# Decode step with cached attention and a gated mixer: the query weights loaded as two halves on two DMA queues

## The chip, the cores and the metric

One core of a Trainium2 chip runs the kernel. The metric is the time of one execution on the device in microseconds; less is better. The engines are named by their tasks: TensorE (PE in the profile) multiplies matrices, VectorE (DVE) and ScalarE (ACT) work on elements, GpSimd (POOL) does small copies, and SyncE (SP) issues loads. SyncE and ScalarE each have a DMA queue of their own (q1 and q10 in the profile); both are served by the same 16 DMA engines of the core.

## The reference

One token, x of 1024 values, goes through two branches, and a scalar gate mixes them:

```
g = sigmoid(sum(x * gate_w))
q = x @ wq                               # wq 1024 x 4096: 32 heads of 128
a = softmax(q k^T / sqrt(128)) v @ wo    # 4 K/V heads, 65536 cached keys each; wo 4096 x 1024
z = gelu(x @ w_in)                       # w_in 1024 x 3584, split into z1 and z2
b = (z1 * (w_sp * layernorm(z2) + b_sp)) @ w_out     # w_out 1792 x 1024
out = g * a + (1 - g) * b
```

All inputs are bfloat16. The K and V caches are 64 MiB each (4 x 65536 x 128 values of two bytes); with the weights the kernel reads 162 MB.

## The kernel before

**Storage.** All big inputs go through one ring in on-chip memory: five slots of 16384 columns on 128 partitions (SUB = 16384; a column is one bfloat16). Slots 0 to 2 hold blocks of K, the last two, from column VB on, hold wq, then w_in, then w_out, then blocks of V; at the end wo takes the place of all.

**The stream.** `load` enters a transfer into the list `stream`, with the keys by which it is used, its place in the ring and its source. The list begins with wq (one load, 32768 columns: on each partition eight rows of wq, one behind the other, 64 KB), the K blocks 0 and 1 (one load of the same size), w_in (28672 columns, in the place of wq), K blocks 2 and 3, w_out, and then K and V by turns.

**The order of the issues.** `issue` walks along the list and stops at the first transfer whose place in the ring has not been used up. `done(key)` marks a transfer as used, and calls `issue` again. All transfers of the list are put on SyncE's queue, in the order of the list (line 389), and each has a semaphore. Four small loads, x, gate_w, w_sp and b_sp, are issued by ScalarE (`small`, line 288). `Recorder` works out from each step's reads and writes which semaphores it must wait for. Where a step waits, all later steps on its engine wait behind it. At the end, `emit` moves SyncE's first two loads (`R.ahead = 2`) and ScalarE's first four (`R.early = 4`) ahead of the barrier with which the program starts.

**The work around the change.** TensorE first transposes x (line 432), spreads w_sp and b_sp over the partitions (line 437), and sums for the gate (line 444). Then one step of 64 matmuls (lines 454 to 465; the instructions have lines 260 and 262) forms q from xT and wq. VectorE copies the result (line 467); two short steps (lines 471 and 479) and copies on VectorE (lines 474 and 482) turn it, and GpSimd writes it to qpad (line 490). From then on the loop over K blocks runs: each block is transposed by VectorE in four pieces (line 502) and multiplied with qpad on TensorE. VectorE's program has the transposes of K block 0 behind the copy of line 482. The issue of w_in stands on SyncE behind the end of the projection, since w_in takes the place of wq; every later load stands behind w_in.

Of the kernel before, what the change touches and what calls it, by code (L numbers as in the profile page):

```python
# [138 lines left out]
def bass_gated_mix__gqa_block_cached__mixer_gmlp__decode_kernel(  # L139
# [29 lines left out]
    SUB = 16384  # L169
# [15 lines left out]
    OFF = {}  # L185
# [16 lines left out]
    arena = nc.alloc_sbuf_tensor("arena", [128, NA], BF16)  # L202

    def ab(name, n, o=0):
        return arena[:, OFF[name] + o:OFF[name] + o + n]

    def af(name, n, o=0):
        return arena[:, OFF[name] + 2 * o:OFF[name] + 2 * (o + n)].bitcast(F32)
# [8 lines left out]
    xT, wb, wbb, oneb = ab("XT", KC), ab("WB", 2), af("WBB", 2), ab("ONEB", 128)  # L217
# [30 lines left out]
    ob, mb, fb = obt[:, :], mbt[:, :], fbt[:, :]  # L248
# [5 lines left out]
    R = Recorder()  # L254
    P = R.op

    def mm(e, loaded, *a, **kw):

        if not loaded:
            return e.matmul(*a, **kw)  # L260
        with nc.discard():
            one = e.matmul(*a, **kw).ins  # L262
        return e.add_instruction(dataclasses.replace(one, name=nc.get_next_instruction_name(), ldweights=False))
# [21 lines left out]
    def small(dst, src, key):  # L285
        def f(e):
            with nc.allow_non_contiguous_dma(reason="a few bytes"):
                return e.dma_start(dst, src)  # L288
        P("ACT", f, w=[key], dma="l" + key)
# [12 lines left out]
    stream = []  # L302
# [1 line left out]

    GRAN = 1024

    def load(keys, src, off):

        n = len(stream)
        w = src.shape[1]  # L310
        for i, key in enumerate(keys):
            place[key] = (n, off + i * (w // len(keys)), w // len(keys))
        stream.append((keys, off, src))

    def rows(w, i, c):

        return w[128 * c * i:128 * c * (i + 1), :].rearrange("(p c) n -> p (c n)", c=c)
# [9 lines left out]
    WQ_N = HQ * Dh  # L327
    VB = KR * SUB

    def load_k(n, slot):  # L330
        load([("k", n)], kv(A_k_cache, n), slot * SUB)

    def load_k2(n, slot):
        load([("k", n), ("k", n + 1)], kv(A_k_cache, n, True), slot * SUB)

    def load_v2(n, off):
        load([("v", n), ("v", n + 1)], kv(A_v_cache, n, True), off)

    load([("wq", 0)], rows(A_wq, 0, 8), VB)
    load_k2(0, 0)  # L340
    load([("win", 0)], rows(B_w_in, 0, 8), VB)
    load_k(2, 2)
# [22 lines left out]
    def store():  # L365
        P("SP", lambda e: e.dma_start(out[0, 0].rearrange("(q n) -> q n", n=QW), osrc), r=["orow"],
          w=["out"], dma="out")
# [5 lines left out]
    def grains(off, w):  # L373
        return list(range(off // GRAN, (off + w + GRAN - 1) // GRAN))

    def issue():

        while issued[0] < len(stream):
            n = issued[0]
            keys, off, src = stream[n]  # L380
            w = src.shape[1]
            gr = grains(off, w)
            if any(k not in used for x in gr if x in owner for k in owner[x]):
                return
            for j, x in enumerate(gr):
                owner[x] = (keys[j * len(keys) // len(gr)],)
            if n == len(stream) - 1:
                store()
            P("SP", lambda e, o=OFF["RING"] + off, w=w, src=src: e.dma_start(arena[:, o:o + w], src),  # L389
              w=[("slot", x) for x in gr], dma="s%d" % gr[0])  # L390
            issued[0] += 1

    def use(key):
        n, off, w = place[key]
        assert n < issued[0], key
        return arena[:, OFF["RING"] + off:OFF["RING"] + off + w], [("slot", x) for x in grains(off, w)]

    def done(key):
        used.add(key)
        issue()  # L400

    issue()


# [8 lines left out]
      r=["m32"], w=["sel"])  # L413
    P("DVE", lambda e: e.tensor_reduce(mq, vw(idf, 0, [[1, 16], [16, 8]]), AXX, ALU.add), r=["idf"], w=["mq"])
    P("DVE", lambda e: e.tensor_reduce(mhalf, vw(idf, 0, [[32, 2], [64, 2], [1, 32]]), mybir.AxisListType.XY, ALU.add),
      r=["idf"], w=["mhalf"])
# [4 lines left out]
    for fe in range(4):  # L421
        P("POOL", lambda e, fe=fe: e.tensor_copy(vw(sele, 128 * fe, [[32, 4], [1, 32]]),
                                                vw(idb, 64 * (fe // 2) + fe % 2, [[0, 4], [2, 32]])),
          r=["idb"], w=[KSE])
# [5 lines left out]
    def f(e):  # L430
        for c in range(KC):
            ins = e.matmul(tb[:, c:c + 1], vw(xm, c, [[8, 128]], 0, 8), oneb[0:8, 0:1], start=(c == 0),  # L432
                           stop=(c == KC - 1), skip_group_check=True)
        return ins
    P("PE", f, r=["xm", "oneb"], w=[KTB])
    P("DVE", lambda e: e.tensor_copy(xT, tb[:, 0:KC]), w=["xT", KTB])
    P("PE", lambda e: e.matmul(mb[:, 0:2], oneb[0:1, :], wb[0:1, :], start=True, stop=True),  # L437
      r=["oneb", "wsp", "bsp"], w=["mb"])
# [6 lines left out]
      r=["ones", "gs"], w=[KTB])  # L445
# [4 lines left out]
      r=["g"], w=["omg"])  # L450
    P("DVE", lambda e: e.tensor_scalar(mhalf, mhalf, col(C_G), None, op0=ALU.mult), r=["mhalf", "g"], w=["mhalf"])


    wqs, keys = use(("wq", 0))

    def f(e):
        for c in range(KC):
            for cg in range(4):
                for s in range(2):
                    o = WQ_N * c + 512 * (4 * s + cg)  # L460
                    ins = mm(e, s > 0, ob[32 * cg:32 * cg + 1, 512 * s:512 * (s + 1)], xT[:, c:c + 1], wqs[:, o:o + 512],
                                   start=(c == 0), stop=(c == KC - 1), tile_position=(0, 32 * cg),
                                   skip_group_check=True)
        return ins
    P("PE", f, r=["xT"] + keys, w=["ob"])
    done(("wq", 0))
    P("DVE", lambda e: e.tensor_copy(psb[0:97, :], ob[0:97, :]), w=["psb", "ob"])  # L467

    def f(e):
# [306 lines left out]
    store()  # L776

    R.ahead = 2
    R.early = 4
    R.emit(nc)  # L780


# [26 lines left out]
```

## Time and profile before

| | |
|---|---|
| median of 3 runs | 381.89 us (381.82 to 381.96) |
| the profiled execution | span 380.3 us from its first to its last instruction; no other time is recorded for it, and the median lies 1.6 us above the span |
| read from memory | 162.01 MB, 426 GB/s over the span |
| SyncE's DMA queue | 98.9% of 16 engines' span |
| ScalarE's DMA queue | 36 packets |
| TensorE, VectorE, ScalarE, GpSimd busy | 62%, 54%, 6%, 2% |

The busy shares are means over the span. The share of a DMA queue is the time that its packets took on the 16 DMA engines. "Issue to landing" of a load is the time from the issuing instruction to the moment at which its semaphore has its full count. Brackets behind an instruction give the idle time of its engine before it, and what ended that.

### The profile page before, as it was taken

How to read it: one execution, taken by the hardware profiler on the slowest of the kernel's cores; microseconds unless marked ns; L12 is line 12 of the kernel's file. 1: busy time of each engine (PE TensorE's matmuls, PEld its weight loads, DVE VectorE, ACT ScalarE, POOL GpSimd, SP SyncE). 2: the span in 40 equal slices, each digit the busy share in tenths (PEclk: the TensorE clock that was granted, in tenths of full speed). 3: DMA queues.
4: the chain of work that ended last, by engine and by line, in shares of the span. 5: the costliest groups of instructions: out<-in, count | busy, mean ns of one | idle time of the engine just before them, and what ended most of it. 6: DMA issues, size and time to landing. Idle time of an engine off the chain costs nothing.

```text
span 380.3 us, 2581 instructions
## 1 busy us (share of the span) xinstructions
PE 235.1 (62%) x1449; PEld 58.1 (15%) x836; DVE 204.6 (54%) x162; ACT 23.3 (6%) x24; POOL 8.4 (2%) x37
## 2 busy tenths in 40 slices
PE   0061388458558924895788138952895884739378
PEld 0010011011111200122112001220121110212015
DVE  4011496778389525965892249745774882312020
ACT  1000000010420000002200000022000000220000
POOL 5000000000000000000000000000000000000000
PEclk9998599696859985998699859995899697958689
DMA  9999999999999999999999999999999999999996
GB/s 435 427 420 400 469 388 438 441 469 431 401 414 441 441 443 427 434 410 424 477 441 434 434 434 414 415 441 441 434 407 433 445 441 441 436 403 424 419 426 262
DMA packets 4254, 162.17 MB, mean 426 GB/s; under 512 B 532, under 2 KB 532, under 8 KB 788
## 3 DMA queue, kind: packets, MB, share of 16 engines
q1 hardware_dynamic: 4208, 162.01, 98.9%
q8 instruction: 9, 0.15, 0.2%
q10 hardware_dynamic: 36, 0.00, 0.0%
q14 instruction: 1, 0.01, 0.0%
HBM read 162.01 MB, written 0.00 MB: 426 GB/s over the span
## 4 chain that ended last, share of the span: by engine, by line
DMA 56%; PE 23%; DVE 18%; ACT 1%; issue 1%; SPq 0%; ACTq 0%; DVEq 0%
DMA arena<-in_A_k_cache_dram 34%; DVE arena L502 15%; DMA arena<-in_A_wo_dram 10%; DMA arena<-in_A_v_cache_dram 8%; PE scp L260 7%; PE scp L262 6%; DMA arena<-in_B_b_sp_dram 5%; PE obt L260 4%; PE obt L262 4%; DVE arena L539 1%; PE fbt L712 1%; PE fbt L660 1%; ACT arena L534 1%; SPq L389 0%; ACTq L288 0%
## 5 line engine op out<-in xcount | busy, mean ns | idle before, releaser
L502 DVE STREAM_TRANSPOSE arena<-arena 128x2048 f32<-128x2048 f32 x64 | 143.0, 2284 | 48.2 <-DMA arena<-in_A_k_cache_dram 32.7
L260 PE MATMUL scp<-arena 128*128 128x512 bf16 (+1 forms) x275 | 112.8, 429 | 87.7 <-DVE arena L502 86.3
L262 PE MATMUL scp<-arena 128*128 128x512 bf16 (+1 forms) x279 | 113.1, 427 | 0.0
L260 PE MATMUL obt<-arena 128*64 128x512 bf16 (+2 forms) x334 | 62.9, 419 | 17.5 <-DMA arena<-in_A_v_cache_dram 17.5
L262 PE MATMUL obt<-arena 128*64 128x512 bf16 (+2 forms) x334 | 62.2, 414 | 0.0
L260 PEld LDWEIGHTS scp<-arena 128*128 128x128 bf16 (+1 forms) x275 | 27.7, 104 | 200.1 <-issue 101.3
L539 DVE STREAM_TRANSPOSE arena<-arena 128x2048 bf16<-128x2048 bf16 x7 | 16.2, 2311 | 28.5 <-PE obt L262 26.4
L534 ACT ACTIVATE arena<-arena 128x2048 bf16<-128x2048 f32 x8 | 16.0, 2002 | 218.6 <-DVE arena L531 195.6
L260 PEld LDWEIGHTS obt<-arena 128*64 128x64 bf16 (+1 forms) x334 | 18.3, 113 | 70.7 <-issue 56.1
L519 DVE TENSOR_SCALAR_CACHE_REDUCE arena<-scp 128x2048 f32<-128x2048 f32 x8 | 18.3, 2292 | 16.0 <-PE scp L262 16.0
L580 PE MATMUL mbt<-arena 128*128 128x128 bf16 x16 | 1.9, 258 | 12.6 <-DVE arena L575 12.6
L542 DVE STREAM_TRANSPOSE arena<-arena 128x1024 bf16<-128x1024 bf16 x2 | 2.5, 1246 | 12.7 <-PE obt L262 12.7
L490 POOL COPY arena<-arena 32x32 bf16<-32x32 bf16 x16 | 3.2, 203 | 234.5 <-PE scp L262 209.7
L568 DVE RECIPROCAL arena<-mbt 128x1 f32<-128x1 f32 x4 | 0.6, 139 | 14.1 <-PE mbt L563 14.1
L531 DVE TENSOR_REDUCE arena<-mbt 128x1 f32<-128x32 f32 x4 | 0.8, 192 | 13.5 <-PE mbt L528 13.5
L437 PE MATMUL mbt<-arena 1*128 1x2 bf16 x1 | 0.2, 158 | 12.3 <-DMA arena<-in_B_b_sp_dram 12.3
L439 DVE COPY arena<-mbt 128x2 f32<-128x2 f32 x1 | 0.2, 160 | 12.3 <-PE mbt L437 12.3
L775 DVE CAST arena<-fbt 36x128 bf16<-36x128 f32 x1 | 0.3, 283 | 11.0 <-PE fbt L712 11.0
L432 PE MATMUL scp<-arena 8*128 8x1 bf16 x8 | 0.7, 199 | 8.7 <-DVE arena L427 8.7
L712 PE MATMUL fbt<-arena 128*32 128x128 bf16 x128 | 4.1, 220 | 0.1
L712 PEld LDWEIGHTS fbt<-arena 128*32 128x32 bf16 x128 | 3.6, 97 | 1.6 <-DMA arena<-in_A_wo_dram 0.8
L467 DVE CAST arena<-obt 97x1024 bf16<-97x1024 f32 x1 | 1.2, 1225 | 4.9 <-PE obt L262 4.9
(91 smaller groups left out, 54.2 us busy)
## 6 DMA issues: line engine op xcount, KB each, us to landing
arena<-in_A_k_cache_dram SPq DMA_DIRECT2D x6, 4096.0 KB, 33.1
arena<-in_A_v_cache_dram SPq DMA_DIRECT2D x2, 4096.0 KB, 26.0
arena<-in_B_w_in_dram SPq DMA_DIRECT2D x1, 7168.0 KB, 30.4
arena<-in_A_wo_dram SPq DMA_DIRECT2D x3, 2048.0 KB, 33.4
arena<-in_B_w_out_dram SPq DMA_DIRECT2D x1, 3584.0 KB, 21.5
arena<-in_A_wo_dram SPq DMA_DIRECT2D x1, 1280.0 KB, 30.3
arena<-in_A_wo_dram SPq DMA_DIRECT2D x1, 512.0 KB, 31.0
arena<-in_A_wo_dram SPq DMA_DIRECT2D x1, 256.0 KB, 30.8
```

What stands on the lines that cost most here:

```text
L260: return e.matmul(*a, **kw)
L262: one = e.matmul(*a, **kw).ins
L467: P("DVE", lambda e: e.tensor_copy(psb[0:97, :], ob[0:97, :]), w=["psb", "ob"])
L490: P("POOL", lambda e, pb=pb: e.tensor_copy(vw(qpad, 24 + 32 * pb, [[QP, 4], [1, 8]], 32 * pb, 32), vw(qall, 8 * g, [[32, 4], [1, 8]], 32 * ...
L502: P("DVE", lambda e: e.transpose(ktb(i).bitcast(F32), sl[:, 4096 * p:4096 * (p + 1)].bitcast(F32)), r=keys[4 * p:4 * p + 4], w=[("kt", i % ...
L519: P("DVE", lambda e: e.tensor_scalar(scs(j), scp[:, :], 0.0, None, op0=ALU.add, op1=ALU.max, accum_out=maxc[:, j:j + 1]), w=[("sc", j % 2) ...
L534: P("ACT", lambda e: e.activation(psb2, scs(j), ACTF.Exp, bias=gcol(j // 2, K_NB), scale=SCALE, accum_out=lp[:, j:j + 1]), r=[("sc", j % 2 ...
L539: P("DVE", lambda e: e.transpose(ptsb2, psb2), r=["psb"], w=[("ptsb", 0), ("ptsb", 1)])
L542: P("DVE", lambda e: e.transpose(ptsb(n), ab("PSB", 1024, 1024 * (n % 2))), r=["psb"], w=[("ptsb", n % 2)])
L580: ins = e.matmul(mb[:, 0:128], sel[:, 128 * c:128 * (c + 1)], osc[:, 128 * c:128 * (c + 1)], start=(c == 0), stop=(c == 3))
L660: ins = e.matmul(fb[32 * b:32 * (b + 1), 0:QW], e4z[0:97, 31 - j:63 - j], part[0:97, QW * s:QW * (s + 1)], start=(first and s % (NW // 2) ...
L712: ins = e.matmul(fb[32 * b:32 * (b + 1), 0:QW], ovz[:, z:z + 32], sl[:, o:o + QW], start=False, stop=(i == 3 and c == 7), tile_position=(0 ...
```

## The change

The load of wq becomes two loads, each of half of the columns that a partition holds: the first four rows of wq on a partition (32 KB), and the next four. The first is issued by SyncE as before, at the head of its queue, followed by K blocks 0 and 1. The second is issued by ScalarE, behind its four small loads; `R.early` becomes 5, so that it too stands ahead of the barrier. The projection reads one half or the other according to the chunk `c`, remains one step, and waits for both halves.

```
-    def load(keys, src, off):
+    def load(keys, src, off, eng="SP"):
...
-        stream.append((keys, off, src))
+        stream.append((keys, off, src, eng))
...
-    load([("wq", 0)], rows(A_wq, 0, 8), VB)
+    for i, eng in enumerate(("SP", "ACT")):
+        load([("wq", i)], rows(A_wq, 0, 8)[:, SUB * i:SUB * (i + 1)], VB + SUB * i, eng)
...
-            P("SP", lambda e, o=OFF["RING"] + off, w=w, src=src: e.dma_start(arena[:, o:o + w], src),
+            P(eng, lambda e, o=OFF["RING"] + off, w=w, src=src: e.dma_start(arena[:, o:o + w], src),
               w=[("slot", x) for x in gr], dma="s%d" % gr[0])
...
-    wqs, keys = use(("wq", 0))
+    wqs, keys = zip(*(use(("wq", i)) for i in range(2)))
...
-                    o = WQ_N * c + 512 * (4 * s + cg)
-                    ins = mm(e, s > 0, ob[32 * cg:32 * cg + 1, 512 * s:512 * (s + 1)], xT[:, c:c + 1], wqs[:, o:o + 512],
+                    o = WQ_N * (c % 4) + 512 * (4 * s + cg)
+                    ins = mm(e, s > 0, ob[32 * cg:32 * cg + 1, 512 * s:512 * (s + 1)], xT[:, c:c + 1], wqs[c // 4][:, o:o + 512],
...
-    P("PE", f, r=["xT"] + keys, w=["ob"])
+    P("PE", f, r=["xT"] + keys[0] + keys[1], w=["ob"])
     done(("wq", 0))
+    done(("wq", 1))
...
-    R.early = 4
+    R.early = 5
```

More of the change, by code (lines that the diff above doesn't have):

```diff
@@ L379, in issue @@
             n = issued[0]
-            keys, off, src = stream[n]
+            keys, off, src, eng = stream[n]
             w = src.shape[1]
```

## The prediction

> **What bounds the kernel now.** I read the page first: shares, queues, the chain's totals. From the table of DMA queues and the lines on HBM traffic:
>
> ```profile
> DMA  9999999999999999999999999999999999999996
> ...
> q1 hardware_dynamic: 4208, 162.01, 98.9%
> ...
> HBM read 162.01 MB, written 0.00 MB: 426 GB/s over the span
> ```
>
> q1 is SyncE's queue. Its packets fill the core's 16 DMA engines for 98.9% of the span, while TensorE is busy 62% and VectorE 54%. The bound is the stream of 162 MB. The chain's DMA share of 56% is smaller only because the chain steps through instructions that release buffers while the stream runs anyway. An edit therefore costs time where it leaves the DMA engines without work, and saves time only where it takes idle time out, and 98.9% leaves little to take.
>
> Second, the timeline of the first 42 us, where the change sits (columns: start us, duration us, engine, line, what; in brackets the idle time before it and what ended it):
>
> ```profile
> 0.00 0.37 SPq L389 DMA_DIRECT2D arena<-in_A_wq_dram  x1
> 0.12 0.56 ACTq L288 DMA_DIRECT2D arena<-in_A_x_dram  x1
> 0.42 0.42 SPq L389 DMA_DIRECT2D arena<-in_A_k_cache_dram  x1
> ...
> 1.34 0.27 ACTq L288 DMA_DIRECT2D arena<-in_B_b_sp_dram  x1
> ...
> 7.42 1.22 DVE L427 TENSOR_TENSOR arena<-arena 8x1024 bf16<-8x1024 bf16 x1 [1.92 <-DMA arena<-in_A_x_dram]
> ...
> 21.67 0.16 PE L437 MATMUL mbt<-arena 1*128 1x2 bf16 x1 [12.32 <-DMA arena<-in_B_b_sp_dram]
> ...
> 28.93 0.33 SPq L389 DMA_DIRECT2D arena<-in_B_w_in_dram  x1
> ...
> 31.40 0.29 DVE L482 CAST arena<-scp 128x128 bf16<-128x128 f32 x1 [0.43 <-PE scp L479]
> ```
>
> ```profile
> 41.32 4.50 DVE L502 STREAM_TRANSPOSE arena<-arena 128x2048 f32<-128x2048 f32 x2 [9.63 <-DMA arena<-in_A_k_cache_dram]
> ```
>
> Two things are to be seen. The next big load, w_in, is issued at 28.93, when the projection's last matmul has ended; until then SyncE's queue holds only wq and the first K block, and that block lands at 41.32. So w_in waits in the queue for about 12.4 us: this is the cover. And bsp, two bytes, is issued at 1.34 and lands only at 21.5 (the chain gives it 20.19 us), while x, issued 1.2 us earlier, lands at 7.42.
>
> Third, the DMA view of the window from 0 to 42 us, which says why:
>
> ```profile
> q1 hardware_dynamic: 304, 17.69, 99.0%
> q10 hardware_dynamic: 36, 0.00, 0.1%
> ...
> arena<-in_B_w_in_dram SPq DMA_DIRECT2D x1, 7168.0 KB, 30.4
> ...
> arena<-in_A_wq_dram SPq DMA_DIRECT2D x1, 21.9
> ```
>
> q10 is ScalarE's queue. wq and the K block have 128 rows of 64 KB each; 304 packets are their 256 rows, 16 small ones for each of the two loads, and the first 16 of w_in. So a packet is one row of a load, and each engine has 8 of them from each big load. The 36 of q10 are twice 8+8+1+1: one for each row of x, gate, wsp and bsp, and one more behind each. A 64 KB packet takes (41.32-21.9)/8 = 2.43 us on an engine. From x to bsp lie six packets of q10 on the engine that carries bsp (two each of gate, wsp, bsp) and 21.53-7.42 = 14.1 us: 2.35 us for each. So an engine takes one packet of SyncE's queue, then one of ScalarE's, by turns, however small the latter is, and one engine (call it E0) carries a part of all four small loads: eight turns.
>
> **The change, part by part.** *SyncE.* The wq load shrinks from 64 KB to 32 KB a row and the K block moves up behind it. The count of SyncE's instructions is unchanged.
>
> *ScalarE.* One more load is issued behind the four small ones, at about 1.65 us for 0.37 us (the wq row). The first ScalarE work is the table load at 2.12; even 0.4 us more there is nothing, as its next work waits 19.8 us for TensorE. If that cover were gone it would cost these 0.4 us.
>
> *TensorE.* The same 64 matmuls in one step, now behind two semaphores ahead of the first matmul. The first half is not used early, so the step starts when the later half lands. Behind it stand the whole of TensorE's program, VectorE's L467, and on SyncE the w_in issue with every later load.
>
> *When the later half lands.* Take E0, with packets of 1.21 us (32 KB) and 2.42 us (64 KB). SyncE's first half needs 8 x 1.21 = 9.7 us, and its eight turns alternate with the eight packets of the small loads, so bsp is down at about 12 us instead of 21.5. Only then does ScalarE's half of wq begin on E0, and its opponent is now the K block: eight turns of 1.21 + 2.42 = 3.63 us, 29.0 us in all. 12 + 29 = 41. So the second half lands together with the K block, at about 41.3: the engine's bytes are the same as before, and the K block's landing does not move. An engine without small packets is done with wq at about 22 to 24 us, one with those of x and gate (four turns) at about 31; E0 is last and decides. The turn order leaves one uncertainty: if the last wq packet, with its small one, is through a turn sooner, ahead of the last K packet, it is 41.3-2.4 = 38.9. I take 41.3: before, bsp needed all eight turns, ending at 21.5 beside wq's own end at 21.9, and the same phase puts wq's end behind the eighth K packet.
>
> *What is late next.* The projection begins at 41.3 instead of 23.08, and the gate's chain (L437 to L444, 1.4 us, which now holds up the projection) is long done. From the first projection matmul to the w_in issue it is 28.93-23.08 = 5.85 us, with a slow first 4.2 us (0.43 us a matmul, later 0.22) that I keep: the first scoring matmuls at 43.77 also start slow for 4.2 us after idling. So w_in is issued at 47.15, when the DMA engines have stood empty since about 41.3. An issue into an empty queue needs time too: wq landed 21.9 us after issue, against 19.4 for the K block, the same bytes behind it: 2.5 us. w_in then takes what it took from the K block's landing on, 28.93+30.4-41.32 = 18.0 us, and lands at 47.15+2.5+18.0 = 67.65 against 59.33: 8.3 us late. Some of the 2.5 us is a spread between engines that the old 18.0 us also holds; with 2.0 it is 7.8. I take 8.1.
>
> *Does it stay?* Projection start to the end of L482 is 8.6 us, so the first K transposes start at 49.95 instead of 41.32: the consumers are 8.6 us late, the stream 8.1. The later loads are issued well ahead: the K issue at 79.62 is 7.7 us before w_out lands (65.81+21.5), the V issue at 99.59 about 7.1 us before the K block ahead of it lands (87.3+19.4); 0.5 us of relative delay fits. With the engines 98.9% full nothing later can give time back, as that needs faster transfers, not earlier issues. The same holds to the last wo load, behind which the tail is unchanged. So the whole 8.1 us reaches the end.
>
> The sum: the profiled span 380.3 + 8.1 = 388.4; the median of 381.89 lies 1.6 above the span, so 390.0.
>
> **A rule beside the rows.** The Trainium skill, "DMA: Bandwidth & Descriptors", section "Queues, rings and completion order", says that an engine goes round between queues packet by packet, and puts a typical packet at some 9 to 17 descriptors. The taking of turns agrees with the 2.35 us above; the size does not. If a turn were all nine descriptors of a load, x would have had to wait for all of wq and land near 21.9, and here it landed at 7.42, with a packet per row. By turns of nine the engine would do SyncE's half (9.7 us), x, the K block (19.4), and then, with SyncE's queue empty, the other small ones and ScalarE's half (9.7): again an end near 41 and a sum near 390, but with the K block down at about 31, ahead of wq; by single rows they land together.
>
> The same page, "Rules for kernel authors", speaks against the change as a way to bandwidth: loads from several issuing engines share the same DMA engines, and only issue time is saved. By that rule alone the sum would be no change, 381.9.
>
> **The rivals.**
>
> *No gap (not slower).* An engine shares by bytes, or E0 does not carry all four small loads. By bytes, ScalarE's half on E0 starts at 12 and goes at half rate: 2 x 9.7 = 19.4 us, landing at 31.4. It decides at 41.32-2.5-5.85 = 33.0: a landing before that leaves w_in queued in time, and the time stays 381.9. The consumers would start at 31.4+8.6 = 40.0, still ahead of the K block. Against it: two bytes took 20.19 us, which sharing by bytes would not do, and eight turns of 2.43 us fit that best. 9%.
>
> *One turn earlier.* The second half lands at 38.9; w_in is issued at 44.75 and lands 5.9 us late instead of 8.3. With the same half-microsecond doubt 5.4 to 5.9, so 387.3 to 387.8. 18%.
>
> *More than the gap.* The stream of smaller packets or the late consumers cost another 1 to 2 us, for instance a K or V issue that misses its turn because VectorE's backlog of eight transposes starts 8.6 us late: 391 to 392. Against it the 7 us that those issues are ahead. 8%.
>
> *Faster.* bsp lands 9 us earlier, which takes 1.4 us out ahead of the projection, and a better fill of the engines at the start might save some. The first has no worth, as the K block at 41.32 rules; the second is at most what is missing to 100% in the window, about 0.4 us of 42. 3%.
>
> The forecast itself, 389.4 to 390.6, has 62%.
>
> **How the numbers follow.** A difference of 0.2% (0.8 us) is about what the measurement can tell from none. Slower by more: 62+18+8 = 88%. Within: the 9% without a gap, less 1 for rounding up the faster case: 8%. Faster: 4%. The range runs from the earlier turn less half a microsecond, 386.8, to 391.6, into the case of more than the gap; it leaves out the cases without a gap and the outer part of the last, under 20%.
>
> **What would show it.** In the profile after: bsp lands at about 12 us and L437 runs there; the first projection matmul starts at 41 us, ended by a wait for wq; w_in is issued at about 47; the DMA share falls to near nothing between 41.5 and 48.5; the first transposes start at about 50; and every later landing is 8 us late. If the projection starts at 39 the turn was one earlier; before 33 and with no hole in the DMA row, I am wrong about the turns; a hole of 7 us without a longer span would mean that the stream has slack which 98.9% does not show.

## The result and the profile after

The changed kernel takes 390.0 us (median of 5 runs, 389.75 to 390.2), the one before 381.89 us (381.68 to 381.96) beside it: 1.0214 times as long, 95% interval 1.0204 to 1.0225. The forecast was 390.0 us. The span of the profiled execution grew from 380.3 to 388.7 us.

From the page of the changed kernel, the DMA row of the 40 slices (9.7 us each), the queues and the traffic:

```profile
DMA  9999289999999999999999999999999999999996
...
q1 hardware_dynamic: 4208, 157.82, 94.4%
q10 hardware_dynamic: 180, 4.20, 2.5%
...
HBM read 162.01 MB, written 0.00 MB: 417 GB/s over the span
```

The same bytes are read; 4.2 MB of them, ScalarE's half of wq, now go over q10. The row that was all nines has a 2 in its fifth slice, 39 to 49 us: the stream stops once, and nowhere else. Its place is seen in the timeline (start, duration, engine, line, what; idle time before, and what ended it):

```profile
1.75 0.36 ACTq L390 DMA_DIRECT2D arena<-in_A_wq_dram  x1
...
11.97 0.16 PE L438 MATMUL mbt<-arena 1*128 1x2 bf16 x1 [4.24 <-DMA arena<-in_B_b_sp_dram]
...
46.78 0.33 SPq L390 DMA_DIRECT2D arena<-in_B_w_in_dram  x1
...
49.25 0.29 DVE L484 CAST arena<-scp 128x128 bf16<-128x128 f32 x1 [0.43 <-PE scp L481]
49.46 4.50 DVE L504 STREAM_TRANSPOSE arena<-arena 128x2048 f32<-128x2048 f32 x2
```

b_sp (the prediction's bsp) is down at 11.8 us instead of 21.5, w_in goes out at 46.78 instead of 28.93, and the first K transposes start at 49.46 instead of 41.32, and no longer wait for a load: the K block had landed at 41.1. The chain of work that ended last has the half itself, and it has the first matmul of the projection right behind it:

```profile
1.75 39.14 DMA arena<-in_A_wq_dram
40.89 0.14 issue
41.03 0.60 PE obt L260 x4
```

Issued at 1.75, ScalarE's half lands at 40.9. The hole is in the windows of 2 us (the last two columns are the share of the DMA engines and GB/s, each packet being counted in the window in which it starts):

```profile
41.00:43.00 2.00, 1.97 (x20) 0.40 (x12) 0.00 (x0) 0.00 (x0) 0.00 (x0) 1.00 0.00 0
43.00:45.00 2.00, 2.00 (x24) 0.42 (x12) 0.00 (x0) 0.00 (x0) 0.00 (x0) 1.00 0.00 0
45.00:47.00 2.00, 1.72 (x32) 0.18 (x8) 0.22 (x1) 0.00 (x0) 0.00 (x0) 1.00 0.00 0
```

For six microseconds TensorE works (first column of busy time) and no packet starts. By the times of the single packets in the trace no DMA engine is busy from 40.7 to 47.7 us. The DMA view gives how long each load took from issue to landing:

```profile
arena<-in_B_w_in_dram SPq DMA_DIRECT2D x1, 7168.0 KB, 20.4
...
arena<-in_A_wq_dram SPq DMA_DIRECT2D x1, 4096.0 KB, 18.1
arena<-in_A_wq_dram ACTq DMA_DIRECT2D x1, 4096.0 KB, 39.1
```

Two loads of the same size, issued 1.75 us apart, land at 18.1 and 40.9 us. w_in lands at 46.78 + 20.4 = 67.2 us instead of 59.3: 7.9 us late. The K load issued at 79.62 before is issued at 87.46, the V load at 107.27 instead of 99.59, and the first loads of wo at 337.99 instead of 330.07: everything behind the hole is issued 7.7 to 8.0 us late to the end, but for one V load, which goes out 10.0 us late (220.81 instead of 210.77) without delaying what follows. In this execution another 0.4 us comes in the last part (the output is stored at 387.45 instead of 379.10); the medians differ by 8.1 us, and I don't read more into that 0.4.

### The profile page after: what moved, and what is told of

Read it like the earlier page. It is cut to its first block, busy times and chain, and to the rows that moved or that the text cites. A ratio compares the mean times of both kernels' runs of the same rounds, so it can differ in the third digit from the quotient of the medians.

```text
span 388.7 us, 2583 instructions
## 1 busy us (share of the span) xinstructions
PE 234.1 (60%) x1449; PEld 58.1 (15%) x836; DVE 204.4 (53%) x162; ACT 23.2 (6%) x24; POOL 9.3 (2%) x37
## 4 chain that ended last, share of the span: by engine, by line
DMA 65%; DVE 17%; PE 17%; issue 1%; ACTq 0%; SPq 0%; DVEq 0%
DMA arena<-in_A_k_cache_dram 38%; DVE arena L504 15%; DMA arena<-in_A_wq_dram 10%; DMA arena<-in_A_v_cache_dram 9%; DMA arena<-in_A_wo_dram 8%; PE scp L260 5%; PE scp L262 4%; PE obt L260 3%; PE obt L262 3%; DVE arena L541 1%; PE fbt L714 1%; ACTq L288 0%; DVE arena L577 0%; DVE arena L575 0%; SPq L390 0%
## 5 line engine op out<-in xcount | busy, mean ns | idle before, releaser
L504 DVE STREAM_TRANSPOSE arena<-arena 128x2048 f32<-128x2048 f32 x64 | 143.0, 2284 | 35.7 <-DMA arena<-in_A_k_cache_dram 22.1
L260 PE MATMUL scp<-arena 128*128 128x512 bf16 (+1 forms) x275 | 111.1, 420 | 75.8 <-DVE arena L504 75.5
L262 PE MATMUL scp<-arena 128*128 128x512 bf16 (+1 forms) x279 | 110.5, 415 | 0.0
L260 PE MATMUL obt<-arena 128*64 128x512 bf16 (+2 forms) x334 | 64.1, 425 | 47.1 <-DMA arena<-in_A_wq_dram 27.6
L262 PE MATMUL obt<-arena 128*64 128x512 bf16 (+2 forms) x334 | 63.5, 422 | 0.0
L582 PEld LDWEIGHTS mbt<-arena 128*128 128x128 bf16 x16 | 1.1, 114 | 13.6 <-DVE arena L577 13.6
## 6 DMA issues: line engine op xcount, KB each, us to landing
arena<-in_B_w_in_dram SPq DMA_DIRECT2D x1, 7168.0 KB, 20.4
arena<-in_A_wq_dram SPq DMA_DIRECT2D x1, 4096.0 KB, 18.1
```

The costliest lines, as they stand in the source:

```text
L504: P("DVE", lambda e: e.transpose(ktb(i).bitcast(F32), sl[:, 4096 * p:4096 * (p + 1)].bitcast(F32)), r=keys[4 * p:4 * p + 4], w=[("kt", i % ...
L582: ins = e.matmul(mb[:, 0:128], sel[:, 128 * c:128 * (c + 1)], osc[:, 128 * c:128 * (c + 1)], start=(c == 0), stop=(c == 3))
```

## The experiments

The theory: a DMA engine takes one packet, that is one row of a load, of each queue by turns. On the engine that carries all four small loads, ScalarE's half stands behind eight tiny packets, each of which costs it one of SyncE's packets, and then shares turns with K packets of twice its size. So it lands with the K block, and the issue of w_in, which hangs on it, comes after the engines have run out of work. Rivals: the split or the smaller rows cost by themselves; two queues with big loads slow the stream; engines share by bytes; the late projection costs through VectorE and TensorE. Each experiment is the changed kernel with one edit, unless it says otherwise; the kernel before, run beside them, took 381.8 to 381.9 us.

### The split without the second queue

```
-    for i, eng in enumerate(("SP", "ACT")):
+    for i, eng in enumerate(("SP", "SP")):
...
-    R.ahead = 2
-    R.early = 5
+    R.ahead = 3
+    R.early = 4
```

> Both halves of wq on SyncE's queue, one behind the other, ahead of the K block; the four small loads alone on ScalarE's. Theory of turns (ScalarE's half stands behind eight small packets on one DMA engine and then shares turns with the K block): wq lands at 21.5 to 22 us as before, no hole, 381.9 us within 0.5; bsp lands at about 12 us, because SyncE's packets are now 32 KB. Rival, the smaller packets or the two loads cost by themselves: something between 382.5 and 390.

Measured: 381.84 us, ratio 0.9999 (0.9990 to 1.0008). The projection's first matmul starts at 21.75 us and b_sp's matmul at 12.02. The split and the smaller rows cost nothing; they even let b_sp through early. So the loss does not come without the second queue.

### The small loads on SyncE's queue

The four small loads go to the head of SyncE's queue; the halves stay on two queues.

```
...
-    small(xrow[0:8, 0:128], A_x[0, 0].rearrange("(i n) -> i n", i=8), KX)
+    small(xrow[0:8, 0:128], A_x[0, 0].rearrange("(i n) -> i n", i=8), KX, "SP")
...
-    R.ahead = 2
-    R.early = 5
+    R.ahead = 6
+    R.early = 1
```

> The halves on two queues as in the change, but the four small loads go to the head of SyncE's queue, so that ScalarE's queue holds only its half of wq. Theory of turns: the half no longer stands behind eight small packets, both halves land by 22 to 24 us, w_in is issued by 30 us, no hole, 381.9 us within 0.5. Rival, two queues with big loads at once slow the stream or the half is late because ScalarE's queue is slow to start: the loss stays, 388 to 390.

Measured: 381.86 us, ratio 1.0000 (0.9991 to 1.0010). From its timeline:

```profile
22.09 0.60 PE L260 MATMUL obt<-arena 128*1 128x512 bf16 x4 [9.75 <-DMA arena<-in_A_wq_dram]
...
28.26 0.33 SPq L390 DMA_DIRECT2D arena<-in_B_w_in_dram  x1
```

Two queues with 4 MB each at once are as fast as one. What costs in the change is what stands ahead of the half in its own queue. Nor is it faster: the rule of the Trainium skill, "DMA: Bandwidth & Descriptors", section "Rules for kernel authors", that loads spread over issuing engines share the same DMA engines and gain no bandwidth, agrees with this 381.86.

### Fewer small packets ahead: six and four turns

b_sp, and in the second kernel w_sp too, are issued by GpSimd. The edit of the first of the two:

```
...
-    small(wb[0:1, 1:2], B_b_sp.rearrange("(a n) -> a n", a=1), "bsp")
+    small(wb[0:1, 1:2], B_b_sp.rearrange("(a n) -> a n", a=1), "bsp", "POOL")
...
-    R.early = 5
+    R.early = 4
```

> The change with one small load, b_sp, issued by GpSimd instead of ScalarE, so that six small packets instead of eight stand ahead of ScalarE's half on the engine that carries them all. Theory of turns: each turn fewer brings the landing forward by one 64 KB packet, 2.42 us, so 40.9 - 4.85 = 36.0 us; w_in is issued at 41.9 instead of 46.8 and the loss falls from 8.1 to about 3.2 us: 385.1 us, within 0.7. Rival, the loss hangs on two queues or on small packets as such: 389 to 390.

> The change with two small loads, w_sp and b_sp, issued by GpSimd, so that four small packets stand ahead of ScalarE's half on the engines that carry x and gate_w. Theory of turns: 40.9 - 4 x 2.42 = 31.2 us for the landing of wq, w_in issued at about 37, before the hole opens; 381.9 us within 0.6. Eight, six and four turns then give losses of 8.1, 3.2 and 0. Rival, the loss falls in proportion to the small packets: four turns would still lose half of it, 386.

Measured: 385.04 us with six turns (ratio 1.0084, 1.0069 to 1.0099), 381.84 us with four (1.0002, 0.9993 to 1.0012). The timeline of six, then of four:

```profile
36.13 0.60 PE L260 MATMUL obt<-arena 128*1 128x512 bf16 x4 [20.11 <-DMA arena<-in_A_wq_dram]
...
41.93 0.33 SPq L390 DMA_DIRECT2D arena<-in_B_w_in_dram  x1
```

```profile
31.60 0.60 PE L260 MATMUL obt<-arena 128*1 128x512 bf16 x4 [10.72 <-DMA arena<-in_A_wq_dram]
...
37.31 0.33 SPq L390 DMA_DIRECT2D arena<-in_B_w_in_dram  x1
```

The projection starts at 41.03, 36.13 and 31.60 us with eight, six and four turns: 4.9 and 4.5 us for two turns each, or 2.3 to 2.45 us a turn, where a 64 KB packet takes 2.43. The loss goes 8.1, 3.2, 0: not in proportion, since it begins only where w_in's issue is too late, and 2 bytes moved to another queue are worth 5 us here. With four turns the projection starts 8.5 us later than in the kernel before (31.60 instead of 23.08 us), and this costs nothing: w_in is out in time, and the transposes wait for the K block anyway.

### Smaller K packets

K blocks 0 and 1 as two loads of 32 KB a row; the small loads are back on ScalarE.

```
-    load_k2(0, 0)
+    load_k(0, 0)
+    load_k(1, 1)
...
-    R.ahead = 2
+    R.ahead = 3
```

> The change with K blocks 0 and 1 as two loads of 32 KB a row instead of one of 64 KB; same bytes, same queues, same small loads. Theory of turns, a turn being one packet of whatever size: on the slowest engine ScalarE's eight packets now alternate with eight of 32 KB, 11.8 + 8 x 2.42 = 31.2 us, so wq lands at about 31, before the 33.0 from which a hole opens; w_in is issued at about 37, no hole, 381.9 us within 0.5. Rival, the engine shares by bytes or time, so the size of the K packets makes no difference: wq still lands at 41 and the time stays at 390.

Measured: 381.98 us, ratio 1.0004 (0.9995 to 1.0013).

```profile
31.63 0.60 PE L260 MATMUL obt<-arena 128*1 128x512 bf16 x4 [17.93 <-DMA arena<-in_A_wq_dram]
...
37.07 0.33 SPq L391 DMA_DIRECT2D arena<-in_B_w_in_dram  x1
```

With the same bytes in both queues, halving the rows of the one brings the other's landing forward by 9.4 us (31.2 expected, 31.5 found). The engines take turns by packets, not by bytes; the rival that would have saved the change is out.

### The half first, the small loads behind it

ScalarE issues its half of wq and then x, gate_w, w_sp and b_sp, whose lines are moved down.

```
...
     issue()
+    small(xrow[0:8, 0:128], A_x[0, 0].rearrange("(i n) -> i n", i=8), KX)
...
+    small(wb[0:1, 1:2], B_b_sp.rearrange("(a n) -> a n", a=1), "bsp")
```

> The change with ScalarE's half of wq issued first and the four small loads behind it. Theory of turns: both halves land by about 22 us, but the eight small packets now share turns with the K block's eight packets of 64 KB, so b_sp lands at about 40 to 41; the step that spreads it stands ahead of the projection on TensorE, so the projection starts at about 42 and the loss is as large as in the change or up to 1.4 us larger: 390 to 391.5 us. Rival, the loss comes from the size of ScalarE's half or from splitting it off, and not from what stands last in ScalarE's queue: 382.

Measured: 391.2 us, ratio 1.0250 (1.0233 to 1.0267). Both halves are down at 22.1 us (22.0 us from issue to landing), and yet:

```profile
41.30 0.16 PE L438 MATMUL mbt<-arena 1*128 1x2 bf16 x1 [12.74 <-DMA arena<-in_B_b_sp_dram]
...
47.74 0.33 SPq L383 DMA_DIRECT2D arena<-in_B_w_in_dram  x1
```

Now the two bytes of b_sp land at 41.2, and their matmul stands ahead of the projection. The four small loads land at 26.6, 31.5, 36.3 and 41.2 us: one comes 4.8 to 4.9 us behind the other, the time of two packets of the K block. So with eight small packets in ScalarE's queue what stands last there lands with the K block (41.3 us here), be it 4 MB or 2 bytes.

### The projection in two steps

Each step takes one half and waits for that half alone, so that 32 matmuls run early.

```
-    P("PE", f, r=["xT"] + keys[0] + keys[1], w=["ob"])
+    for half in range(2):
...
+        P("PE", f, r=["xT"] + keys[half], w=["ob"])
```

> The change with the projection in two steps, each waiting for its own half of wq. Theory: wq still lands at 40.9 us; only 32 matmuls are left then, all at the slow pace of 0.43 us for four, 3.4 to 3.7 us instead of 5.75, so w_in is issued at about 44.5 and the loss falls by 2.1 to 2.4 us: 387.6 to 388.0 us. Rival, the loss does not come from the wait for w_in's issue: 390.

Measured: 387.84 us, ratio 1.0159 (1.0144 to 1.0174). The first step starts at 18.11, the second at 41.10:

```profile
18.11 0.60 PE L260 MATMUL obt<-arena 128*1 128x512 bf16 x4 [4.48 <-DMA arena<-in_A_wq_dram]
...
41.10 0.60 PE L260 MATMUL obt<-arena 128*1 128x512 bf16 x4 [19.41 <-DMA arena<-in_A_wq_dram]
...
44.52 0.33 SPq L390 DMA_DIRECT2D arena<-in_B_w_in_dram  x1
```

w_in goes out at 44.52: 2.26 us sooner than in the change, and the time is 2.2 us less. A microsecond of delay of that issue is a microsecond of the end. Issues at 41.93 (six turns), 44.52 and 46.78 us cost 3.2, 6.0 and 8.1 us; followed back at one for one, the loss is zero at about 38.7, some 2.5 us before the K block lands, which agrees with the price of a restart that the prediction used.

### A block of K ahead of w_in: three kernels that tell less than hoped

K block 2 is put ahead of w_in on SyncE's queue, to keep the engines busy while the projection is late: with the change, with the change and two steps, and with the kernel before.

```
-    load([("win", 0)], rows(B_w_in, 0, 8), VB)
     load_k(2, 2)
+    load([("win", 0)], rows(B_w_in, 0, 8), VB)
```

> The change, with K block 2 (4 MB, its slot is free) put ahead of w_in on SyncE's queue. Theory: ScalarE's half still lands late, at about 41 us or later by what the K block's packets add, but 9.7 us of work stand in the queue when w_in is issued at about 47, so the engines do not run empty: 381.9 to 382.7 us although the projection starts 18 us later than before the change. Rival, the late projection itself costs (VectorE and TensorE late with blocks 0 and 1): 388 to 391.

> K block 2 ahead of w_in and the projection in two steps, both together. The K-first kernel alone closed the hole at 41 to 49 us and still lost 4.5 us, with the engines nearly empty at 86 to 88 and short of work at 106 to 108 us. Theory: there the consumers were 8.4 us late with the stream on time, more than the 7.1 and 7.7 us by which those loads were issued ahead before; two steps make the consumers 2.2 us earlier, about 6.2 us late, so both loads are issued in time (by 0.9 us or more, less some 1 us to restart): 381.9 to 383 us. Rival, the loss of the K-first kernel comes from something else (the new order of the blocks, the halves): 386.

> The kernel before, wq whole on SyncE's queue, with nothing changed but K block 2 put ahead of w_in. It tells what of the two K-first kernels' loss is the late projection and what the new order. Theory A, the order costs by itself: w_in lands 9.7 us later, at 69.0 us, the mixer's first step waits for it on TensorE and the transposes of K block 2 stand behind that on VectorE, about 5.3 us later than before (74.4 instead of 69.08); the K load issued at 79.62 before goes out at 84.9 and the V load at 105.1, as in the kernel with K first and two steps, and the time is the same as there: 384.4 us, within 0.6. Theory B, it was the late projection alone: w_in is issued at 29 us, the projection is early, 381.9 us.

Measured: 386.41 us with the change (ratio 1.0115, 1.0094 to 1.0135), 384.38 with two steps (1.0067, 1.0052 to 1.0082), 387.17 with the kernel before (1.0140, 1.0123 to 1.0157). All three expectations missed. The hole at 41 us did close in the first (DMA share 0.76 or more in each window of 2 us from 41 to 49), but others opened, which its windows show:

```profile
84.00:86.00 2.00, 2.00 (x10) 0.40 (x5) 1.89 (x2) 0.00 (x0) 0.00 (x0) 1.00 0.73 315
86.00:88.00 2.00, 1.49 (x7) 0.29 (x3) 1.64 (x5) 0.32 (x2) 0.00 (x0) 1.00 0.03 14
...
106.00:108.00 2.00, 1.45 (x24) 0.19 (x6) 1.97 (x3) 0.51 (x1) 0.55 (x3) 1.00 0.30 131
```

The 0.30 at 106 us says little by itself, since the kernel before has such a window too, at 88 us, with no engine idle; by the times of the packets the engines stand idle here for 2.2 us between 82 and 92 us and for 0.5 us between 104 and 112 (means over the 16).

After the first of them I blamed the late projection. The kernel before with the same order says otherwise: its projection is early, and it loses more, 5.4 us. Its timeline:

```profile
52.53 0.33 SPq L389 DMA_DIRECT2D arena<-in_A_k_cache_dram  x1
...
69.17 0.55 PE L260 MATMUL obt<-arena 128*1 128x448 bf16 x4 [5.93 <-DMA arena<-in_B_w_in_dram]
...
74.44 0.33 SPq L389 DMA_DIRECT2D arena<-in_B_w_out_dram  x1
74.44 1.09 DVE L614 COPY arena<-obt 128x896 f32<-128x896 f32 x1 [8.87 <-PE obt L262]
75.57 1.11 DVE L616 STREAM_TRANSPOSE arena<-arena 128x896 f32<-128x896 f32 x1
76.60 4.46 DVE L502 STREAM_TRANSPOSE arena<-arena 128x2048 f32<-128x2048 f32 x2
...
87.19 0.33 SPq L389 DMA_DIRECT2D arena<-in_A_k_cache_dram  x1
```

w_in lands 9.7 us later, the mixer's first step waits for it, and runs 5.3 us where it took 3.3 before (62.56 to 65.81; TensorE had idled for 5.9 us and began at its slow pace). The transposes of K block 2 stand behind that step and behind two more of VectorE's (2.2 us, which the kernel before had done before that block landed): they start at 76.60 instead of 69.08, 7.5 us late, while w_out, the end of the stream at that time, lands at 87.5 as before (87.3). In the three kernels the mixer's step ends at 74.22, 72.27 and 74.44 us, the K load of 79.62 goes out at 87.11, 84.93 and 87.19, that is 7.5, 5.3 and 7.6 us late, and they lose 4.5, 2.5 and 5.4 us.

So the order itself makes the consumers late while the stream is on time. In the first and the last the delay eats up the 7.7 us by which that load had been issued ahead of the landing of w_out, and nothing is left for the restart. In the second 2.4 us are left, about the price of a restart, and it still loses 2.5 us. The idle time of the DMA engines around these places, 2.7, 1.4 and 2.6 us, is only about half of each loss. In the last the packets themselves took some 2 us longer in all (q1 98.0% of a span of 385.9 us, against 98.9% of 380.3); why stays open. These kernels don't price the projection at 41 us by itself either; only that 8.5 us of its delay cost nothing was seen, with four turns.

## Why the prediction was right

*The landing of the second half*: 41.3 forecast, 40.9 found, by the sum of eight small turns and eight turns with the K block. By the times of the packets one engine alone carries ScalarE's rows after 29 us: they start at 18.71, 22.34, 25.96, 29.58, 33.21 and 36.83 us, one every 3.62, the length of a 32 KB and a 64 KB packet. The last row ends at 38.0; the packet of 4 bytes behind it, which completes the load, has a turn of its own and starts at 40.45, behind the eighth K row, as the prediction chose against "one turn earlier". From 38.1 to 41.5 us it is all that q10 has:

```profile
q1 hardware_dynamic: 23, 0.46, 31.4%
q10 hardware_dynamic: 1, 0.00, 0.0%
```

The dose of turns (2.3 to 2.45 us each) and the K rows of 32 KB (31.5 us) show the mechanism, which the prediction had from a two-byte load that took 20.19 us. The two other readings are out: by bytes the smaller K rows would have changed nothing, and "one turn earlier" would have started the projection at 39.

*Projection to issue*: 5.85 us forecast, 46.78 - 41.03 = 5.75 found. *Issue to landing of w_in*: 2.5 + 18.0 = 20.5 forecast, 20.4 found. *w_in late by* 8.1 (between 7.8 and 8.3) forecast, 7.9 found. That the total agrees to the tenth is luck: the last part of this execution is 0.4 us longer than the shift, which no term of the sum had, and the median lies 1.3 us above the profiled span where the sum had 1.6.

*The rest shifts as a whole*: confirmed, the K and V issues of the argument 7.8 and 7.7 us late against a stream 7.9 us late. The consumers came 8.1 us late (49.46 instead of 41.32) where 8.6 were forecast, so only 0.3 us of relative delay had to fit, and did. The K-first kernels show that this step had less room than its text claims: the prediction put the reserve at about 7 us and named no price for using it, and there 5.3 us of relative delay went with a loss of 2.5. "About 7 us ahead" was no measure of what can be afforded.

*A detail that was wrong, without consequence*: engines without small packets were to end wq at 22 to 24 us. SyncE's half landed at 18.1 us, which fair turns from the start would not allow (2 x 9.7 = 19.4 and the start), so ScalarE's half began later on those engines too. The DMA view of the first 6.8 us has q10 at 37 packets:

```profile
q1 hardware_dynamic: 72, 2.36, 89.0%
q10 hardware_dynamic: 37, 0.17, 6.0%
```

32 of the 37 are those of x and gate_w, so five rows of the half, 0.17 MB, had begun five microseconds after its issue. The slowest engine did not feel it.

*The rule that was weighed*: the Trainium skill, "DMA: Bandwidth & Descriptors", section "Queues, rings and completion order", has engines go round between queues packet by packet, with 9 to 17 descriptors in a typical packet. The turns are as it says; their size is not. In these loads a packet was a row, whether of 2 bytes or of 64 KB, as the projection's starts at 36.13, 31.60 and 31.63 us show.

## What to carry to other kernels

Before putting a big load on a second queue, look at what stands ahead of it there: where engines take turns by packets, each tiny packet costs a whole packet of the other queue, so count packets and not bytes to find the landing (40.9 us here behind eight small ones, 19.5 behind none, with the small loads on SyncE's queue). Where the stream is the bound, price such a landing at the next issue that hangs on it, not at the engine that waits: the loss is zero up to the moment at which the queue would run empty, and one for one beyond it. And when loads are put in another order to fill a hole, follow the consumers in their program order: the three kernels with K first opened new holes and lost more than these explain.

## What was not expected of the hardware

A load behind four small ones in ScalarE's queue hardly began in the first 5 us after its issue, even on DMA engines that carried none of them (0.17 MB by 6.8 us; its first packet starts at 6.6, 4.8 us after the issue). It is not ScalarE's queue as such: with the small loads on SyncE's queue the half there, behind the same four, first moves at 5.4 us, 4.1 after its issue, while the half alone on ScalarE's queue moves 1.0 us after its own. What in the small loads holds up the next one is not known.
